# Attention's weighted sum with the values as the stationary operand, and the division by the weights' sums put off until x is loaded

## The chip, the cores and the metric

The kernel runs on one core of a Trainium2 chip. The metric is device time in microseconds of one execution; the kernel before has a median of 813.89 us over three runs (812.94 to 816.54). Engines are TensorE (PE), VectorE (DVE), ScalarE (ACT), GpSimd (POOL) and SyncE (SP), which issues nearly all DMA transfers.

## The reference

Block-sparse attention over 4 batches, 8 heads, 768 positions and 64 values a head, and then a two-layer MLP on the joined heads (3072 tokens, 512 to 2048 to 512). Cut to what matters:

```
scores = scale * q @ k.T                       # scale = 1/8
mask: own block of 32 and its neighbours, first and last block, 3 sampled blocks per query block
      (queries of the first and the last block see every key)
attn = exp(scores - max);  attn = attn / (sum(attn) + 1e-9)
x = (attn @ v), heads side by side             # (3072, 512)
h = x @ w_in;  r = max(h, 0);  g = s * r * r + b;  out = g @ w_out
```

The MLP works on numbers split in a high and a low part, with three products for one.

## The kernel before

**Slots.** The attention runs over 52 slots in the order `T["ORD"]`, two batches (a and b) at a time. An "s" slot is four heads against one tile of 128 queries; its keys are 256 local and global ones (the static part) and, for each block of 32 queries, three sampled blocks (the sampled part). There are 40 of them. A "d" slot (8) does the first and last query block, with all 768 keys, for two pairs of heads; an "h" slot (4) does the half tile that is left at the end of a batch, for all eight heads. A unit is one tile of weights within a slot: four to an "s" or "h" slot, two to a "d" slot.

**Work of a slot.** PE makes scores (L710, L724, sampled L736). DVE adds the mask and takes the maximum (L751), ACT exponentiates and leaves the sum of each row in `dn` (L763). PE transposes the weights (L787), DVE and ACT in turn copy them out of PSUM (L791, L793). PE multiplies with the values: static part L832 ("d" L821, "h" L826), sampled part L846. Here the transposed weights are the stationary operand, 64 queries of them in the static part and 32 in the sampled one, and 64 columns of V move, so that the result has queries on partitions. `x_scale` (L852, DVE) multiplies it by the reciprocals that `recip` (L766) made of the slot's sums; `x_transpose` (L858, PE) turns it, two 128x128 pieces for an "s" or "h" slot and one for a "d" slot; `x_copy` (L863, ACT) takes it out of PSUM, and `spill` (L875) stores it to `xd` in DRAM. The result and its transpose share one PSUM bank, of which there is one for all slots; seven others hold scores and transposed weights.

**The order.** Class `Plan` holds each step of the attention, of the decoding of the weights w_in and w_out (64-bit words, nine steps on DVE and ACT for a block, L75 to L85) and of the first 30 MLP sub-steps as an op with an engine, a cost, a priority and its dependencies. `Plan.order` simulates the engines and writes every engine's instructions in the order that comes out; each engine then runs its own queue in that order. The PE sequence of the attention is fixed by `line`: weights' transposes of slot i, x transposes of slot i-1, scores of slot i+2, products of slot i.

**The MLP.** x is held in eight halves of 384 tokens (`g` from 0 to 7, two to a batch). `xload` (L359) brings two 128-row pieces of a half from `xd`, and `xsplit` makes the high part on ACT (L372) and the low part on DVE (L374). A sub-step `(g, f)` is the first layer for 128 hidden columns (L401 to L403, four triples), the square and split of the hidden values (L406 to L419), and two sub-steps later the second layer (L440 to L442). Halves 0 and 1 run first, 2 and 3 from sub-step 32; the sub-steps from 30 on are written in a plain loop, not planned. Halves 4 to 7 are done at the end with seven products instead of eight (L1193); they read x through `get` (L1152).

## Time and profile before

| what | value |
|---|---|
| median of three runs | 813.89 us (812.94 to 816.54) |
| the profiled execution | 807.04 us, span 805.3 us |
| busy: PE, DVE, ACT, POOL | 785.4, 560.9, 493.8, 214.6 us |
| DMA | 95.61 MB, mean 119 GB/s |
| granted PE clock, mean | 0.996 |

The attention fills the span up to about 276 us, the planned sub-steps of the MLP the part up to about 400, the loop the part up to about 540, and the last four halves the rest. Rows give start, length, engine and line, tiles written and read, the number of instructions in brackets or after an x, and in square brackets the idle time before and what ended it. A PE row counts matmuls, a PEld row the loads of the stationary operand, which overlap them. In groups by line the first number behind the bar is busy time in us, the second the mean length of one in ns.

### The profile page before, as it was taken

What the parts mean: (1) busy time and instruction counts of PE and PEld (TensorE: products, weight loads), DVE (VectorE), ACT (ScalarE), POOL (GpSimd) and SP (SyncE); (2) the same over time, 40 slices, a digit from 0 to 9 for tenths busy, and PEclk for the clock granted to TensorE, in tenths of its full rate; (3) what the DMA queues carried; (4) which work ended last, traced back from release to release, by engine and by line L of the source; (5) the groups of instructions that cost most, each with busy time, mean ns of one, the idle gap of its engine ahead of it and who ended that gap; (6) DMA issues with size and microseconds to landing.
All of it is one profiled execution on the core that took longest, in us unless ns stands there. A gap on an engine that the chain in (4) does not pass through costs nothing.

```text
span 805.3 us, 22018 instructions
## 1 busy us (share of the span) xinstructions
PE 785.4 (98%) x8416; PEld 682.0 (85%) x8416; DVE 560.9 (70%) x1379; ACT 493.8 (61%) x1175; POOL 214.6 (27%) x438
## 2 busy tenths in 40 slices
PE   8988999999999999999999999999999999999997
PEld 6677887888887889999889999998899998999996
DVE  4756778888888899999742222278768869766662
ACT  3656778878788788787563433457355457544542
POOL 1732133222400032322323222223223223322321
PEclk9999999999999999999999999999999999999999
DMA  8988897887777433433221010412200012000002
GB/s 257 279 226 294 229 258 214 251 247 222 210 221 230 142 105 105 132 105 109 81 98 40 30 37 27 158 46 78 86 1 7 0 40 95 6 1 0 1 2 78
DMA packets 86073, 95.61 MB, mean 119 GB/s; under 512 B 11344, under 2 KB 64976, under 8 KB 85968
## 3 DMA queue, kind: packets, MB, share of 16 engines
q1 hardware_dynamic: 85968, 94.21, 38.6%
q8 instruction: 66, 1.08, 0.6%
q14 instruction: 39, 0.32, 0.1%
HBM read 77.41 MB, written 12.58 MB: 112 GB/s over the span
## 4 chain that ended last, share of the span: by engine, by line
PE 85%; ACT 4%; DMA 4%; DVE 3%; issue 3%; SPq 1%; POOL 0%; ACTq 0%; DVEq 0%; POOLq 0%
PE m L1193 13%; PE o L441 10%; PE o L442 10%; PE o L440 10%; PE t L787 9%; PE xs L832 5%; PE s L710 5%; PE h L402 5%; PE h L403 5%; PE h L401 5%; PE xs L846 3%; PE s L736 2%; PE s L724 2%; PE xs L858 1%; PE xs L821 1%
## 5 line engine op out<-in xcount | busy, mean ns | idle before, releaser
L419 POOL TENSOR_TENSOR hid<-hid,hid 128x384 fp32r<-128x384 f32 x128 | 139.3, 1089 | 436.5 <-ACT hid L415 253.2
L763 ACT ACTIVATE ptile<-ptile,nm 128x352 f32<-128x352 f32 (+2 forms) x208 | 120.8, 583 | 30.7 <-DVE nm L751 29.7
L1210 ACT ACTIVATE hid<-hid,sb_b,sb_s 128x384 f32<-128x384 f32 x64 | 45.4, 709 | 112.4 <-DVE hid L1204 112.3
L410 DVE SCALAR_TENSOR_TENSOR hid<-hid,sb_s 128x384 f32<-128x384 f32 x64 | 41.5, 649 | 88.4 <-ACT hid L406 88.3
L670 POOL COPY kg<-kt 128x128 f32 x264 | 63.5, 293 | 124.4 <-PE s L736 119.0
L751 DVE CUSTOM_DVE_ANT_0 ptile<-s,ms 128x352 f32<-128x352 f32 x160 | 74.4, 521 | 25.6 <-PE s L736 25.4
L401 PE MATMUL h<-x,win 128*128 128x384 f32 x256 | 86.5, 338 | 0.6 <-ACT hid L406 0.6
L402 PE MATMUL h<-x,win 128*128 128x384 f32 x256 | 86.1, 336 | 0.2 <-DVE x L374 0.2
L403 PE MATMUL h<-x,win 128*128 128x384 f32 x256 | 86.3, 337 | 0.0
L787 PE MATMUL t<-ident,ptile 128*128 128x128 f32 x608 | 79.4, 280 | 0.7 <-ACT ptile L763 0.7
L442 PE MATMUL o<-woutr,hid 128*128 128x512 f32 x192 | 75.9, 395 | 0.0
L442 PE MATMUL o<-wout,hid 128*128 128x512 f32 x192 | 75.9, 395 | 0.0
L441 PE MATMUL o<-wout,hid 128*128 128x512 f32 x192 | 75.8, 395 | 0.0
L441 PE MATMUL o<-woutr,hid 128*128 128x512 f32 x192 | 75.8, 395 | 0.0
L440 PE MATMUL o<-wout,hid 128*128 128x512 f32 x192 | 74.7, 389 | 0.0
L440 PE MATMUL o<-woutr,hid 128*128 128x512 f32 x192 | 74.6, 389 | 0.0
L787 PEld LDWEIGHTS t<-ident,ptile 128*128 128x128 f32 x608 | 65.9, 141 | 6.9 <-ACT ptile L763 1.9
L406 ACT ACTIVATE hid<-h 128x384 f32<-128x384 f32 x64 | 31.1, 486 | 52.3 <-PE h L403 49.2
L414 ACT ACTIVATE hid<-hid,sb_b 128x384 f32<-128x384 f32 x64 | 39.3, 614 | 37.8 <-DVE hid L410 37.8
L791 DVE COPY pt<-t 128x384 f32<-128x384 f32 (+1 forms) x104 | 56.1, 545 | 8.1 <-PE t L787 5.6
L793 ACT COPY pt<-t 128x384 f32<-128x384 f32 (+1 forms) x104 | 48.8, 472 | 20.9 <-PE t L787 20.3
L1193 PE MATMUL m<-xT,wop 128*128 128x384 f32 x288 | 58.5, 337 | 2.6 <-DVE sum L1286 1.5
(169 smaller groups left out, 1650.8 us busy)
## 6 DMA issues: line engine op xcount, KB each, us to landing
vg<-in_v_dram SPq DMA_DIRECT2D x136, 128.0 KB, 3.7
v<-in_v_sta_dram SPq DMA_DIRECT2D x40, 256.0 KB, 4.7
kt<-in_k_seq_dram SPq DMA_DIRECT2D x16, 544.0 KB, 7.0
raw_i<-in_w_in_dram SPq DMA_DIRECT2D x16, 512.0 KB, 4.9
raw_o<-in_w_out_dram SPq DMA_DIRECT2D x16, 512.0 KB, 3.3
v<-in_v_dram SPq DMA_DIRECT2D x16, 384.0 KB, 5.0
xd<-xst SPq DMA_DIRECT2D x44, 128.0 KB, 4.0
out_dram<-ob SPq DMA_DIRECT2D x20, 256.0 KB, 2.1
```

The source lines that it names most:

```text
L401: nc.tensor.matmul(ph, wh, xh, start=(c == 0), stop=False)
L402: nc.tensor.matmul(ph, wh, xl, start=False, stop=False)
L403: nc.tensor.matmul(ph, wl, xh, start=False, stop=(c == NCC - 1))
L419: nc.gpsimd.tensor_tensor(out=htile(5 + i % 3), in0=t, in1=gh.bitcast(F32), op=ALU.subtract)
L440: nc.tensor.matmul(acc, gh[:, tsl], wout(f, 0), start=first, stop=False)
L441: nc.tensor.matmul(acc, gh[:, tsl], wout(f, 1), start=False, stop=False)
L442: nc.tensor.matmul(acc, gl[:, tsl], wout(f, 0), start=False, stop=last)
L670: nc.gpsimd.tensor_copy(kg[:, m], kts[b][:, :, bass.ds(box["js"][m], BLK)])
L751: nc.vector.tensor_tensor_reduce(out=pt[:, :w], in0=sps.pop((n, g))[:, :w], in1=msk, scale=-scale, scalar=FMAX if g == 0 else nm[:, 0:1], ...
L763: nc.scalar.activation(pt[:, :w], pt[:, :w], AF.Exp, bias=nms[n][:, last:last + 1], scale=-1.0, accum_out=dns[i][:, g, j:j + 1])
L787: nc.tensor.transpose(tp[:, c, :], src[:, c * P:(c + 1) * P], ident)
L1193: nc.tensor.matmul(to, w_, x_, start=(c == 0 and k == 0), stop=(c == 1 and k == 2))
```

## The change

In the product with the values the operands change places. V is stationary (64 columns of one head) and the transposed weights move: 128 queries at a time in the static part, 32 in the sampled part, two heads of a pair on the two halves of the output partitions. The result then has the head's values on partitions and queries along the free dimension, as x is stored, and `x_transpose` goes; `x_copy` moves it from PSUM on DVE. A slot's result is not divided. The sums of a batch are gathered in one tile of 52 columns (`sums`); when its last slot has its exponentials, `recip` makes reciprocals of them, PE transposes them, and 48 rows of 128 are stored to `rd` in DRAM. Whoever loads a piece of x also loads the matching factors, repeated over 64 partitions (`rload`: two transfers for an even half, six for an odd one), and `xscale` multiplies in place, 128x768 on DVE. Halves 4 to 7 are loaded, multiplied and stored back to `xd` in sub-steps 34 to 49 (`xback`). The factors for halves 0 and 1, and the raw x of half 1, lie in a tile of their own (`xr`), which takes a turn in the two buffers of the sampled values. The planner's costs are set anew.

```diff
+    def rload(g, c2, t):
+        b, hf = divmod(g, 2)
+        t3 = t.rearrange("p (t c n) -> p t c n", c=2, n=P)
+        nt = HALF // P - hf
+        for par in range(2):
+            to = t3[par * D:(par + 1) * D]
+            o = (24 + par * 8 if hf else par * 12)
+            src = rd[b, o:o + 4 * nt].rearrange("(t x) n -> t x n", x=4)[:, 2 * c2:2 * c2 + 2, :].rearrange("t x n -> t (x n)")
+            nc.sync.dma_start(out=to[:, :nt].rearrange("p t c n -> p t (c n)"), in_=src.unsqueeze(0).broadcast_to([D, nt, 2 * P]))
+            if hf:
+                src = rd[b, 40:48].rearrange("(h r k) (a n) -> r k a h n", r=2, k=2, a=2)[par, c2]
+                for a in range(2):
+                    nc.sync.dma_start(out=to[:, nt, a].rearrange("p (h n) -> p h n", h=2), in_=src[a].unsqueeze(0).broadcast_to([D, 2, D]))
+        rfac[(g, c2)] = t
+    def xscale(g, c2, dst=None):
+        t = xraw[(g, c2)] if dst is None else dst
+        nc.vector.tensor_tensor(out=t, in0=xraw[(g, c2)], in1=rfac[(g, c2)], op=ALU.mult)
+        xraw[(g, c2)] = t
+    def xback(g, c2):
+        nc.sync.dma_start(out=xd[g // 2, g % 2, :, :, 2 * c2:2 * c2 + 2, :], in_=tcn(xraw[(g, c2)]))
...
-                                 accum_out=dns[i][:, g, j:j + 1])
-        def recip(i):
...
+                                 accum_out=sums[slots[i][1]][:, sum_column(n, g):sum_column(n, g) + 1])
+        def recip(b):
+            t = sums[b]
+            nc.vector.tensor_scalar(out=t[:, :NROW], in0=t[:, :NROW], scalar1=1e-9, scalar2=None, op0=ALU.add)
+            nc.vector.tensor_tensor(out=t[:, NROW - 4:NROW], in0=t[:, NROW - 4:NROW], in1=t[:, NROW:], op=ALU.add)
+            nc.vector.reciprocal(t[:, :NROW], t[:, :NROW])
+        def recip_transpose(b):
+            tps[("r", b)] = next_bank(f"r{b}")[:NROW, :P]
+            nc.tensor.transpose(tps[("r", b)], sums[b][:, :NROW], ident)
...
-            hp = 2 * (j % 2) + j // 2
-            for c in range(2):
-                for rows in halves:
-                    nc.tensor.matmul(xs[rows], pt[:, c, rows], vt[:, c, hp * D:(hp + 1) * D], start=(j == 0 and c == 0),
-                                     stop=False, skip_group_check=True)
+            for c in range(2):
                 for par in range(2):
+                    j = 2 * k + par
+                    pt = pts_of[n + j][0]
...
+                        hp = 2 * par + k
+                        to, w, p = xs[halves[par], k], vt[:, c, hp * D:(hp + 1) * D], pt[:, c, :]
+                    nc.tensor.matmul(to, w, p, start=(k == 0 and c == 0), stop=False, skip_group_check=True)
...
-                    nc.tensor.matmul(xs[rows], w, vg[:w.shape[0], m, h * D:(h + 1) * D], start=False, stop=(j == 3),
-                                     tile_position=(0, r * BLK), skip_group_check=True)
+            for k in range(2):
                 for r in range(4):
+                    for par in range(2):
...
+                        nc.tensor.matmul(to, vg[:p.shape[0], m, h * D:(h + 1) * D], p, start=False, stop=(k == 1 and r == 3),
+                                         tile_position=(0, par * D), skip_group_check=True)
-        def x_scale(i):
...
-        def x_transpose(i):
...
-            nc.scalar.copy(xst_of[i], tr)
+            nc.vector.tensor_copy(xst_of[i], xs)
...
-        costs = {"s": (485, 535, 350, 260, 685), "d": (810, 0, 350, 780, 0), "h": (380, 535, 240, 160, 685)}
+        costs = {"s": (485, 535, 350, 470, 640), "d": (810, 0, 350, 1420, 0), "h": (380, 535, 240, 240, 640)}
...
             for c2 in range(2):
                 xload(2, c2)
+                rload(2, c2, scratch("klp", HX, f"r2_{c2}").bitcast(F32))
         mlp1(i)
         if i in (31, 32):
+            for c2 in range(2):
+                xscale(i - 29, c2)
             for c in range(NCC):
                 xsplit(i - 29, c)
         if i == 31:
             for c2 in range(2):
                 xload(3, c2)
+                rload(3, c2, scratch("khp", HX, f"r3_{c2}").bitcast(F32))
...
+        if 34 <= i < 50:
+            m, k = divmod(i - 34, 2)
+            gc = 4 + m // 2, m % 2
+            if k == 0:
+                xload(*gc)
+                rload(*gc, scratch("klp", HX, f"r{gc}").bitcast(F32))
+            else:
+                xscale(*gc)
+                xback(*gc)
```

**PE, the products of one "s" slot.** Before (`v` and `vg` are the static and the sampled values, `pt` the transposed weights, `xs` the result):

```order
L832 MATMUL xs_2434<-v_0_2075,pt_0_2391 64x64 x4
L832 MATMUL xs_2434<-v_0_2075,pt_0_2397 64x64 x4
...
L846 MATMUL xs_2434<-vg_2_1469,pt_0_2391 32x64 x4
L846 MATMUL xs_2434<-vg_2_1469,pt_0_2397 32x64 x4
...
L787 MATMUL t_0_2547<-ident,ptile_81 128x128 x3
L858 MATMUL xs_2434<-ident,xss_2544 128x128 x2
```

Now, with the two heads in turn (8 rows of the first kind, 16 of the second):

```order
L878 MATMUL xs_2009<-pt_0_1973,v_0_1791 64x128
L878 MATMUL xs_2009<-pt_0_1979,v_0_1791 64x128
...
L893 MATMUL xs_2009<-pt_0_1973,vg_2_1366 64x32
L893 MATMUL xs_2009<-pt_0_1979,vg_2_1366 64x32
...
L833 MATMUL t_0_2079<-ident,ptile_81 128x128 x3
```

The sizes are the output's partitions and columns. 16 static products of 64 moving columns have become 8 of 128, 16 sampled ones of 64 columns on 32 partitions have become 16 of 32 columns on 64, and the two transposes behind the next slot's are gone.

**DVE, from the last copies of transposed weights to the first MLP sub-steps.** Before (`win` and `wout` are decoded blocks, `wkhp`, `wklp` and `raw` their steps, `hid` the hidden values):

```order
L791 COPY pt_0_6987<-t_0_6973 128x384
L85 SCALAR_TENSOR_TENSOR win_5488<-wklp_2714,wkhp_2704 128x512
L78 SCALAR_TENSOR_TENSOR wklp_2715<-wklp_2715,raw_i_6167 128x512
L83 TENSOR_TENSOR win_5488<-wkhp_2705,raw_i_6167 128x512
L84 TENSOR_SCALAR wkhp_2705<-win_5488 128x512
L852 TENSOR_TENSOR xss_7033<-xs_7000,rc_6983 128x128
L85 SCALAR_TENSOR_TENSOR win_5488<-wklp_2715,wkhp_2705 128x512
```

Now:

```order
L837 COPY pt_0_6293<-t_0_6280 128x384
L401 TENSOR_TENSOR x_1_6001<-xraw_1_4465,x_0_5857 128x384 x2
L83 TENSOR_TENSOR win_5116<-wkhp_2726,raw_i_5517 128x512
L383 TENSOR_TENSOR xr<-xr 128x768
L901 COPY xst_6339<-xs_6298 128x128
L819 COPY rt_6346<-r_6327 48x128
L383 TENSOR_TENSOR xr<-xr 128x768
L401 TENSOR_TENSOR x_1_6361<-xr,x_0_6341 128x384
L437 SCALAR_TENSOR_TENSOR hid_6359<-hid_6359,sb_s 128x384
L401 TENSOR_TENSOR x_1_6361<-xr,x_0_6341 128x384 x3
```

Two low parts of half 0 and all four of half 1 (L401, before L374), and both multiplies of half 1 (L383), now stand behind the last copy; before, the six low parts stood ahead of it. Up to the first block of `wout` there are five squares in both orders.

**SP, the loads for halves 2 and 3.** Before:

```order
L359 DMA xraw_0_8138<-xd 128x3x256
L359 DMA xraw_1_8140<-xd 128x3x256
L359 DMA xraw_0_8183<-xd 128x3x256
L359 DMA xraw_1_8185<-xd 128x3x256
L451 DMA out_dram<-ob_0_8228 128x512
```

Now, from the last of these loads on:

```order
L362 DMA xraw_1_7530<-xd 128x3x256
L374 DMA r_1_7532<-rd 64x2x256
L378 DMA r_1_7532<-rd 64x2x64 x2
L374 DMA r_1_7532<-rd 64x2x256
L378 DMA r_1_7532<-rd 64x2x64 x2
L478 DMA out_dram<-ob_0_7582 128x512
```

Six transfers of factors have come between the last load of x and the first store of output; the other three loads have two, two and six behind them.

More of the change, by code (lines that the diff above doesn't have):

```diff
@@ L818, in av_static @@
                 for c in range(NCH):
-                    for par in range(2):
-                        rows = halves[par]
-                        nc.tensor.matmul(xs[rows], pt[c // 3][:, c % 3, rows], vt[:, c, rows], start=(c == 0), stop=(c == NCH - 1))
+                    for a in range(2):
+                        for j in range(2):
+                            nc.tensor.matmul(xs[halves[j], a], vst[(i, j)][:, c, halves[a]], pts[j][c // 3][:, c % 3, halves[a]],
+                                             start=(c == 0 and a == 0), stop=(c == NCH - 1 and a == 1), skip_group_check=True)
@@ L849, in x_scale @@
-        def x_scale(i):
-            xs = xs_of.pop(i)
-            xss = xss_of[i] = xp.tile([P, 4, D], F32, tag="xss", name=f"xss{i}")[:, :xs.shape[1], :]
-            nc.vector.tensor_tensor(out=xss, in0=xs, in1=rcs.pop(i).unsqueeze(2).broadcast_to(list(xs.shape)), op=ALU.mult)
-        def x_transpose(i):
-            tr = tr_of[i]
-            xv = xss_of.pop(i).rearrange("p h d -> p (h d)")
-            for pr in range(tr.shape[1]):
-                nc.tensor.transpose(tr[:, pr, :], xv[:, pr * P:(pr + 1) * P], ident)
@@ L1036 @@
         o_t, o_av, ends = last[1][-1], last[2][-1], [y for x in evs.values() for y in x]
-        every = [ac, o_av, *ends]
+        every = [ac, o_av, *ends, rt[len(slots) - 1]]
         op("s", 450, 30, lambda: nc.sync.dma_start(out=sb_s, in_=s_in.rearrange("(a o) -> a o", o=1).broadcast_to([P, 1])))
```

174 lines of the change are left out of this document (95 added, 79 removed).

## The prediction

> **What bounds the kernel now.** I read the page first (busy shares, then the 40 slices), then the chain of waits between 78 and 274 us, then busy time by stage, and last the two places where one stage hands over to the next.
>
> ```profile
> PE 785.4 (98%) x8416; PEld 682.0 (85%) x8416; DVE 560.9 (70%) x1379; ACT 493.8 (61%) x1175; POOL 214.6 (27%) x438
> PE   8988999999999999999999999999999999999997
> DVE  4756778888888899999742222278768869766662
> ```
>
> TensorE (PE) is full from the fourth slice on. VectorE (DVE) is full beside it in slices 15 to 20, about 280 to 400 us. The chain says what PE's time consists of. This is one "s" slot (four heads against 128 queries) of the attention:
>
> ```profile
> 84.43 0.49 PE s L736 x32
> 84.93 1.08 PE xs L832 x32
> 86.01 0.58 PE xs L846 x32
> 86.59 1.46 PE t L787 x12
> 88.05 0.22 PE xs L858 x2
> 88.27 1.06 PE s L710 x8
> ```
>
> Six groups, 4.9 us, no gap: in this stage the other engines' savings are worth nothing, and only PE's own steps count. Before about 78 us it is different; the chain there has pieces like these, in which PE waits for loads:
>
> ```profile
> 34.44 7.30 DMA v<-in_v_dram
> 44.35 4.57 DMA vg<-in_v_dram
> ```
>
> Only 6 of the 40 "s" slots lie there (192 of 1280 records, 32 to a slot):
>
> ```profile
> L832 PE MATMUL xs<-v,pt 128*64 128x64 f32 x192 | 7.2, 226 | 1.0 <-issue 1.0
> ```
>
> In the MLP, PE is busy all 20 us of each stretch, and DVE has 0.6 to 1.9 us left in it (columns: PE, PEld, DVE, ACT, POOL busy):
>
> ```profile
> 300.00:320.00 20.00, 20.00 (x103) 18.21 (x102) 18.11 (x31) 15.51 (x28) 5.57 (x5) 1.00 0.27 82
> 340.00:360.00 20.00, 20.00 (x101) 18.04 (x101) 19.38 (x32) 15.19 (x27) 5.46 (x5) 1.00 0.39 124
> ```
>
> **The step price on PE.** The program has 16 static products to a slot and the trace 32 matmuls with 32 weight loads, so each product is two of each. The old static products alternate between two halves of the array, so 32 are 16 steps. Two groups of the same shape but different count separate the step from what a change of shape costs, and the weight loads show how long one takes:
>
> ```profile
> 263.50 1.55 PE xs L821 x48
> 128.87 0.62 PE xs L826 x16
> 130.07 1.02 PE t L787 x8
> L710 PEld LDWEIGHTS s<-kt,qr_4s 64*128 64x128 f32 x64 | 5.5, 186 | 1.7 <-issue 1.3
> L832 PEld LDWEIGHTS xs<-v,pt 128*64 128x64 f32 x1280 | 40.7, 138 | 7.8 <-issue 1.1 <-ACT ptile L763 0.6 <-ACT pt L793 0.6
> L846 PEld LDWEIGHTS xs<-vg,pt 96*32 96x32 f32 x1280 | 20.2, 109 | 6.0 <-issue 3.3
> ```
>
> 24 steps take 1.55 and 8 take 0.62, so a step is (1.55 - 0.62) / 16 = 0.058 us and a group's fixed part 0.62 - 8 x 0.058 = 0.16. Twelve transposes take 1.46 and eight 1.02, so 128 moving columns cost 0.11, and 64 some 0.055. A load grows from 109 ns at 32 stationary columns to 186 at 128: 0.8 ns a column, so 64 columns occupy about 51 ns. In the old static step load (51) and stream (55) overlap.
>
> **Part 1: the new products.** Static: 8 products with 128 moving columns are 8 steps of 0.11 plus 0.16, 1.04 us instead of 1.08. Sampled: the stationary side is now 64 columns of V and the moving side 32 queries, on two halves instead of four quarters, so 16 steps instead of 8. Each streams 0.11 / 4 = 0.0275 us but loads 64 columns. Bounds: 0.0275 if the loads hide, 0.051 + 0.0275 = 0.079 if nothing overlaps. I take 0.058, the step of the rows that load 64 columns every time: the stream is shorter there, the load is not. That is 16 x 0.058 = 0.93 us, and no fixed part, since static and sampled now have one shape, against 0.58. The two L858 transposes (0.22) go. A slot: 1.08 + 0.58 + 0.22 = 1.88 becomes 1.04 + 0.93 = 1.97, +0.09; 34 slots make +3.1. An "h" slot: 0.62 + 0.58 + 0.22 becomes 0.62 + 0.93, +0.13, four make +0.5. A "d" slot has 24 steps of the same load before and after and loses one transpose: -0.11, and the four late ones make -0.4. Four transposes of the sums: +0.4; the one of the third batch stands right behind the slot whose sums it needs and waits for three small DVE operations, about 0.2 each: +0.6. Sum for PE: **+4.2 us**.
>
> A rule speaks against the sampled half as well: the Trainium skill, TensorEngine Tiling, "Instruction Overhead", says that a matmul with one moving column takes as long as one with 60. By it a step would be 60 / 128 x 0.11 = 0.052 and the sampled group 0.83 us, an estimate, 0.1 below mine; no row here has 32 moving columns.
>
> **Part 2: what leaves DVE and ACT.**
>
> ```profile
> L852 DVE TENSOR_TENSOR xss<-xs,rc 128x256 f32<-128x256 f32 x44 | 18.6, 423 | 7.0 <-PE xs L846 6.9
> L863 ACT COPY xst<-xs 128x256 f32<-128x256 f32 x44 | 16.4, 372 | 17.5 <-PE xs L858 16.0 <-DMA vg<-in_v_dram 0.7 <-DMA v<-in_v_sta_dram 0.3
> L775 DVE RECIPROCAL rc<-rc 128x4 f32<-128x4 f32 x44 | 7.8, 178 | 1.5
> L774 DVE TENSOR_SCALAR rc<-dn 128x4 f32<-128x4 f32 x44 | 7.4, 168 | 0.0
> ```
>
> The multiply of 0.42 becomes a copy of the same shape; ACT's copies and the small reciprocals go, some 16 and 15 us of busy time. All of it lies beside the full PE: worth 0. The copy sits under the next slot's transposes and scores, 1.46 + 1.06 us; without that cover it would cost 0.42 a slot.
>
> **Part 3: the handover to the MLP.** The division comes back as xscale, a 128x768 multiply on DVE, ahead of every split of x. For the second half of batch 0 it comes after the last attention copy, so that six splits and two multiplies stand between it and the first decoded block of w_out, which the first second-layer product needs:
>
> ```profile
> L1166 DVE TENSOR_TENSOR sum<-sum,sum 128x768 f32<-128x768 f32 x6 | 5.7, 950 | 0.0
> 271.60 1.01 DVE L374 TENSOR_TENSOR x<-wout,x 128x384 fp32r<-128x384 f32 x2
> 274.42 0.54 DVE L791 COPY pt<-t 128x384 f32<-128x384 f32 x1
> 290.49 0.69 DVE L85 SCALAR_TENSOR_TENSOR wout<-wklp,wkhp 128x512 fp32r<-128x512 f32 x1
> L83 DVE TENSOR_TENSOR win<-wkhp,raw_i 128x512 fp32r<-128x512 f32 x16 | 12.1, 759 | 1.3 <-ACT wkhp L82 0.7 <-issue 0.4 <-ACT raw_i L79 0.2
> 275.36 1.62 PE L821 MATMUL xs<-v,pt 128*64 128x64 f32 x48
> 287.80 0.44 PE L401 MATMUL h<-x,win 128*128 128x384 f32 x1 [0.60 <-ACT hid L406]
> 291.04 0.40 PE L440 MATMUL o<-wout,hid 128*128 128x512 f32 x1
> ```
>
> Before, DVE needs 291.2 - 275.0 = 16.2 us from the last copy to that block. In the same stretch of the changed order stand six splits more (0.5 each, from the pair that takes 1.01: 3.0), two multiplies (0.95 each: 1.9), and a net half microsecond of decode steps (one L83 more, one L78 for one L84) and of copies: +5.5, so 21.7. PE's cover is the last slot's product (1.55) and first-layer products: before, 26 triples in 291.04 - 276.91, less 0.6 of wait and 0.1 of transpose, so 0.515 each; in the changed order 28 stand ahead. PE is out of work 1.55 + 0.1 + 14.4 = 16.1 us after that product starts, the block is ready 21.7 - 0.4 = 21.3 after: a stall of 5.2 where there were 0.6, **+4.6**. PE cannot make it up, being full afterwards. Bounds: 0 if DVE closes the gaps of its 16.2 us, 7 if the added operations run with the contention that made some there twice as long.
>
> **Part 4: the third and fourth x at sub-steps 31 and 32.** Here the split was just in time:
>
> ```profile
> 407.54 0.52 SPq L359 DMA_DIRECT2D xraw<-xd  x1
> 411.80 0.45 PE L402 MATMUL h<-x,win 128*128 128x384 f32 x1 [0.23 <-DVE x L374]
> win<-xrest SPq DMA_DIRECT2D x30, 128.0 KB, 2.0
> xd<-xst SPq DMA_DIRECT2D x44, 128.0 KB, 4.0
> ```
>
> The load at 407.54 waits for a buffer of the x before. Behind it SP now issues six more transfers for the factors, 0.5 each: the last at 411.4, landed at 413.4 (2.0, as transfers of this quiet stretch) to 415.4 (4.0). On DVE both multiplies stand ahead of all four splits, so the first split ends 0.95 + 0.55 later, at 414.9 to 416.9, and PE waits for it instead of until 411.80; behind it wait the square of that sub-step and, on SP, the output stores, both with microseconds to spare. +3.1 to +5.1, and I take **+3.6**, near the row of the quiet stretch. The eight scalings with write-back from sub-step 34 on fall into slices where DVE is at 2 to 4 tenths, and cost nothing; were DVE full there, they would cost 8 x 0.95.
>
> **Sum.** 4.2 + 4.6 + 3.6 = 12.4 us. The profiled execution took 807.0 us (span 805.3), so 819.4 in its terms. The three timed runs have a median of 813.9, 0.85% above it; taken to the median, 826.
>
> **Rivals.**
> Loads hide (faster): if a load runs ahead under other matmuls, the sampled step is 0.0275, its group 0.44, and a slot loses 0.40: 34 x 0.40 + 4 x 0.36 + 0.4 - 1.0 = 14.4 less on PE, and with parts 3 and 4 a net -6: 808. It decides below a step of about 0.042. For it: load and stream overlap in L832 today. Against it: they overlap one deep, the step there is 0.058 with a load of 0.051, and in the new step nothing is left to overlap with. The Trainium skill, TensorE: Matmul & The Clock Gate, "The mechanism", speaks for this rival: the queue pulls a load ahead of running matmuls where it goes to another part of the array or to the background buffer.
> Only PE's part shows (no change): DVE catches up before the first w_out block, and the factors land in time; +4.2, 818.
> The queue hurts more (slower still): the new order puts one k block and two tiny loads ahead of the v load of the third slot, in the stage where the chain runs through DMA; 3 us there, with the upper bounds 7 and 5.1: +19, 833.
> That the change does not do what it says is excluded by the order of PE's rows: the transposes are gone and the shapes are as described.
>
> **Chances.** Forecast 0.55, loads hide 0.12, only PE's part 0.17, worse 0.16. Faster or slower means by over 0.5%, about 4 us, what a measurement of this kernel can tell: below 809.8 is the first rival alone, 0.12; the second lies at the edge of 818 and counts as no change with a little of the others, 0.18; slower 0.70. Range 808 to 834; the forecast's own is 820 to 831.
>
> **What would show it.** Right: in the chain, the new sampled group at about 0.93 us with 32 records and the static one at 1.04; a period of about 5.0 us; a PE wait of some 5 us for the first w_out block and one of 3 to 5 us at the second x of sub-step 33, named DVE. Wrong: a sampled group of 0.5 us, a DVE that finishes the block within 17 us, or an x split on time. The forecast falls if the sampled step is below 0.042.

## The result

The changed kernel takes 827.13 us (median of 4 runs, 825.7 to 828.67), the kernel before 815.21 (812.94 to 817.32). The ratio is 1.0153 with a 95% interval of 1.011 to 1.0197: slower by about 12 us. The forecast was 826.

The profiled execution of the changed kernel has a span of 824.1 us, 18.8 more than the first profile of before (805.3). A second profile of before, taken later, has 811.9, much nearer to its median. So every place is compared with both. The stretches between fixed points on PE (slots counted from 0 to 51, MLP sub-steps from 0 to 63; the start of the first matmul of each) are, in us:

| stretch | before | before, second profile | changed |
|---|---|---|---|
| start to the scores of slot 7 | 51.3 | 54.9 | 53.3 |
| to the scores of slot 48 | 201.1 | 202.6 | 199.7 |
| to the first layer of sub-step 8 (the handover) | 52.2 | 52.2 | 61.0 |
| to sub-step 32 | 102.45 | 102.45 | 102.45 |
| to sub-step 38 (the joins of the third and fourth x) | 25.6 | 25.6 | 31.95 |
| to sub-step 62 (multiplies with write-back) | 100.5 | 100.5 | 103.45 |
| to the end | 272.1 | 273.7 | 272.2 |

Three stretches are longer, by 8.8, 6.3 and 3.0 us, together 18.1; the attention up to slot 48 is not longer at all in this execution (in others with the same product it is, see experiment 3). The page of the changed kernel shows the first two of them as notches in PE's slices, the 14th with the 15th and the 21st, where before had nines:

```profile
PE 793.1 (96%) x7684; PEld 693.1 (84%) x7684; DVE 568.6 (69%) x1307; ACT 479.9 (58%) x1123; POOL 215.7 (26%) x438
PE   8799999999999879999979999999999999999997
```

**The slot.** The chain of waits of the changed kernel (start, length, group) shows five groups, 4.95 us from the scores of one slot to those of the next (a period below) where before had six groups and 4.90:

```profile
58.33 1.06 PE s L737 x8
59.40 0.49 PE s L763 x32
59.89 1.02 PE xs L878 x16
60.91 0.91 PE xs L893 x32
61.82 1.46 PE t L833 x12
```

**The handover.** PE's timeline (in brackets the idle time ahead and what ended it):

```profile
272.91 0.27 PE L815 MATMUL r<-ident,sums 128*48 128x128 f32 x1 [1.19 <-DVE sums L811]
279.31 0.44 PE L428 MATMUL h<-x,win 128*128 128x384 f32 x1 [0.69 <-DVE rt L819]
293.42 0.45 PE L428 MATMUL h<-x,win 128*128 128x384 f32 x1 [1.35 <-ACT hid L433]
298.48 0.49 PE L467 MATMUL o<-wout,hid 128*128 128x512 f32 x1 [2.71 <-DVE wout L83]
299.67 0.77 PE L468 MATMUL o<-wout,hid 128*128 128x512 f32 x1 [0.69 <-DVE wout L85]
300.24 0.63 PE L469 MATMUL o<-wout,hid 128*128 128x512 f32 x1
300.67 0.63 PE L467 MATMUL o<-wout,hid 128*128 128x512 f32 x1
```

Two of the waits are the sums (their inversion on DVE, and the copy of their transpose, whose bank the first MLP product wants), two are the first block of w_out, and the one of 1.35 us is for a hidden value on ACT. The products behind them start 0.43 us apart instead of 0.23: PE's clock is lower there, 0.61 in the first of the stretches that follow.

**The joins.** In busy time by stretch (PE, PEld, DVE, ACT, POOL, then the granted clock, DMA share, GB/s) both notches end in a piece with a clock of 0.6, with 10 and 13 matmuls where the next piece of the same length has 18 and 22:

```profile
300.00:304.00 4.00, 3.74 (x10) 2.60 (x10) 3.33 (x7) 3.94 (x7) 0.00 (x0) 0.61 0.39 124
304.00:308.00 4.00, 4.00 (x18) 3.31 (x19) 3.93 (x7) 3.08 (x7) 1.30 (x1) 1.00 0.45 132
426.00:430.00 4.00, 3.88 (x13) 3.84 (x14) 2.00 (x5) 3.52 (x9) 0.42 (x1) 0.57 0.43 167
430.00:434.00 4.00, 4.00 (x22) 3.65 (x21) 0.62 (x1) 3.19 (x6) 0.90 (x2) 1.00 0.57 204
```

The second notch is the fourth x, in the timelines of PE, DVE and SP's queue:

```profile
426.12 0.69 PE L429 MATMUL h<-x,win 128*128 128x384 f32 x1 [4.85 <-DVE x L401]
426.92 0.52 PE L428 MATMUL h<-x,win 128*128 128x384 f32 x1
427.24 0.52 PE L429 MATMUL h<-x,win 128*128 128x384 f32 x1
```
```profile
418.65 0.94 DVE L383 TENSOR_TENSOR xraw<-xraw,r 128x768 f32<-128x768 f32 x1
424.63 0.96 DVE L383 TENSOR_TENSOR xraw<-xraw,r 128x768 f32<-128x768 f32 x1 [5.04 <-DMA r<-rd]
425.51 1.96 DVE L401 TENSOR_TENSOR x<-xraw,x 128x384 fp32r<-128x384 f32 x4
```
```profile
417.29 0.54 SPq L362 DMA_DIRECT2D xraw<-xd  x1
420.78 1.81 SPq L378 DMA_DIRECT2D r<-rd  x2
```

SP's load of the second piece waits for a buffer until 417.29; the six transfers of its factors stand behind it, the last landed at 424.63, and all four splits, those of the first piece too, wait on DVE behind the second multiply.

**The multiplies with write-back.** At sub-steps 47 and 49 DVE waits for the factors in the same way and holds up the square that is next in its queue (509.53 in the second case), and PE waits four times, for 0.21 and 0.41 us near 502 and for 0.89 and 0.40 near 512. By the starts of the matmuls around them, which lie 1.2 and 1.8 us further apart than elsewhere, these waits are the whole 3.0 us. The longest is shown last:

```profile
498.45 0.96 DVE L383 TENSOR_TENSOR xraw<-xraw,r(7, 0)_8072 128x768 f32<-128x768 f32 x1 [5.48 <-DMA r(7, 0)_8072<-rd]
508.65 0.96 DVE L383 TENSOR_TENSOR xraw<-xraw,r(7, 1)_8141 128x768 f32<-128x768 f32 x1 [5.97 <-DMA r(7, 1)_8141<-rd]
509.53 0.61 DVE L437 SCALAR_TENSOR_TENSOR hid<-hid,sb_s 128x384 f32<-128x384 f32 x1
```
```profile
511.39 0.50 PE L467 MATMUL o<-woutr,hid 128*128 128x512 f32 x1 [0.89 <-ACT hid L442]
```

### The profile page after: what moved, and what is told of

Same layout as the page of the kernel before. It is cut to its first block, busy times and chain, and to the rows that moved or that the text cites. A ratio compares the mean times of both kernels' runs of the same rounds, so it can differ in the third digit from the quotient of the medians.

```text
span 824.1 us, 20594 instructions
## 1 busy us (share of the span) xinstructions
PE 793.1 (96%) x7684; PEld 693.1 (84%) x7684; DVE 568.6 (69%) x1307; ACT 479.9 (58%) x1123; POOL 215.7 (26%) x438
## 4 chain that ended last, share of the span: by engine, by line
PE 69%; DVE 16%; ACT 5%; DMA 5%; SPq 3%; issue 2%; POOL 0%; DVEq 0%; ACTq 0%
PE m L1246 13%; PE t L833 8%; PE o L469 7%; PE o L468 7%; PE o L467 7%; PE xs L878 5%; PE s L737 5%; PE xs L893 5%; PE s L763 3%; DVE hid L437 2%; PE h L429 2%; PE h L430 2%; PE h L428 2%; DMA kt<-in_k_seq_dram 2%; DVE wkhp L84 2%
## 5 line engine op out<-in xcount | busy, mean ns | idle before, releaser
L441 ACT ACTIVATE hid<-hid,sb_b 128x384 f32<-128x384 f32 x64 | 39.3, 614 | 65.5 <-DVE hid L437 65.5
L437 DVE SCALAR_TENSOR_TENSOR hid<-hid,sb_s 128x384 f32<-128x384 f32 x64 | 44.1, 689 | 47.6 <-ACT hid L433 47.6
L839 ACT COPY pt<-t 128x384 f32<-128x384 f32 (+1 forms) x104 | 48.6, 469 | 39.3 <-PE t L833 38.9
L1246 PE MATMUL m<-win 128*128 128x384 f32 x288 | 55.9, 338 | 0.0
```

The lines of the kernel that those rows point to most:

```text
L1246: nc.tensor.matmul(to, w_, x_, start=(c == 0 and k == 0), stop=(c == 1 and k == 2))
```

## The experiments

The theory after the result: the product costs almost nothing, and the division put off costs nearly all. The rivals: the product or its layout costs; the multiplies' own time costs; the loads cost; the order that the planner wrote costs.

**1. The kernel before once more.** No edit.

> The kernel before, unchanged, profiled a second time. The profiled execution of before took 807.0 us while its timed runs had a median of 815.2; the changed kernel's profiled execution took 825.9 and its median was 827.1. So the profiles differ by 18.8 us and the medians by 11.9. If the first profile of before was a lucky execution, this one has a span near 812 to 815 and shows by name a stretch that is some 8 us longer than in the first (I expect it where the kernel is just in time: the split of x before 411.8 us, where PE waited 0.23 us, and the loads before 78 us). If executions with a profile are simply shorter for this kernel, the span is 804 to 807 again and nothing moves.

Span 811.9, 813.67 us by the clock. The 6.6 us more lie in the loads before slot 7 (3.6), in waits between slots 7 and 48 (1.5 more than in the first profile) and, at the end, in the clock: the same PE wait of 1.5 us near 555 us is followed by a full clock in the first profile of before and by 3.4 us of slow clock in the second (10 matmuls against 17):

```profile
554.00:557.40 3.40, 3.40 (x17) 3.01 (x18) 2.41 (x5) 2.45 (x6) 2.02 (x2) 1.00 0.00 0
```
```profile
559.00:562.40 3.40, 3.35 (x10) 3.06 (x11) 2.43 (x5) 2.56 (x6) 1.89 (x2) 0.57 0.00 0
```

So the first profile of before was a lucky one, and not at the split before 411.8 us, where I had looked for it: that stretch is the same to 0.03 us. The stretches marked 52.2, 102.45, 25.6 and 100.5 repeat so well that they are used below.

**2. Without the division, order kept.**

```diff
     def rload(g, c2, t):
+        return
...
-        nc.vector.tensor_tensor(out=t, in0=xraw[(g, c2)], in1=rfac[(g, c2)], op=ALU.mult)
-        xraw[(g, c2)] = t
+        return
...
-        if 34 <= i < 50:
+        if False:
```

> The changed kernel without the put-off division: no loads of the factors, no multiply of x, no write-back of the scaled x; x stays undivided (so the result leaves the division out). The transposed products stay, and so does the order of everything else. Theory (the put-off division costs 17.4 of the 18.8 us between the two profiles, the transposed product 1.4): first second-layer product at 291 to 293 us instead of 298.5, no PE wait of more than 0.5 us between 415 and 430 and none between 500 and 515, span 806 to 809, and timed 0.98 to 1.00 of before. Rival (the transposed product, its layout in memory or the new order of the loads is what costs): the span stays above 818 and the waits of the changed kernel stay.

Ratio 1.0037 (1.0005 to 1.0069), span 814.6, both above the theory's. The joins are whole again (25.6 and 100.5), as the theory had it. The handover is not: 61.6 us, and the first second-layer product at 296.2. My account of the handover (VectorE has 1.9 us of multiplies and 3.0 of splits more to do) falls as far as the multiplies go. They are gone, and PE waits the same; DVE, in order, now stands waiting for the first square (the first three rows give what PE waited for: us in total, times, longest):

```profile
PE o L467 <- DVE wout L83: 2.7, 1, 2.7
PE h L428 <- ACT hid L433: 1.4, 1, 1.4
PE r L815 <- DVE sums L811: 1.2, 1, 1.2
```
```profile
279.95 0.62 DVE L437 SCALAR_TENSOR_TENSOR hid<-hid,sb_s 128x384 f32<-128x384 f32 x1 [2.50 <-ACT hid L433]
```

**3. Multiplies, but no loads of factors.** In each multiply the second operand is x itself (the result is x squared); `rload` returns at once.

```diff
-        nc.vector.tensor_tensor(out=t, in0=xraw[(g, c2)], in1=rfac[(g, c2)], op=ALU.mult)
+        nc.vector.tensor_tensor(out=t, in0=xraw[(g, c2)], in1=xraw[(g, c2)], op=ALU.mult)
```

> The changed kernel with the multiplies of x and the write-back, but without the loads of the factors: each multiply takes x itself as its second operand (the result is x squared instead of x divided). It parts the DVE work of the put-off division from the loads that it waits for. Theory: the handover (8.1 us in the profile) is DVE work and stays, first second-layer product at 297 to 299 us; the PE wait of 4.85 us at 421 and the waits of 1.7 us at 501 to 512 are loads of the factors, and go: span 813 to 816. Rival (the multiplies themselves, ahead of the splits and of the squares, make all three): the wait at 421 stays above 3 us, those at 501 to 512 stay, span 821 to 824.

Ratio 1.0077 (1.0046 to 1.0108), span 820.8. Handover 61.0, as expected; the joins 26.75, a wait of 1.12 us left of 4.85; sub-steps 38 to 62 back at 100.5. So of the 6.3 us at the fourth x the multiplies make 1.1 and the loads 5.2, and the 3.0 behind are loads alone. The span is 5 us above what I gave, nearly all of it before slot 48: the two periods from the scores of slot 24 to those of slot 26 are together 5.9 us too long. PE waits there for the sampled values:

```profile
141.21 1.28 PE L893 MATMUL xs<-pt,vg 96*64 96x32 f32 x20 [2.44 <-DMA vg<-in_v_dram]
```

The last two loads of these values (issued at 137.3 and 137.9 us) stand behind a store of x in SP's queue; in before they stand ahead of it. And this is not one execution's accident. Over the twelve profiles with the transposed product, these two periods are 2.6 to 6.1 us too long in six, 1.2 to 1.4 in two, and at most 0.7 in four, the changed kernel's own among them; in the two profiles of before it is at most 0.5. So the change has a cost here that comes and goes and that the table above does not show. What decides whether it comes stays open.

**4. Half the stationary columns in the sampled product.**

```diff
-                        nc.tensor.matmul(to, vg[:p.shape[0], m, h * D:(h + 1) * D], p, start=False, ...
+                        nc.tensor.matmul(to[:D // 2], vg[:p.shape[0], m, h * D:h * D + D // 2], p, start=False, ...
```

> The changed kernel with 32 instead of 64 stationary columns of V in each sampled product (the second half of each head's dimensions is left out of the sampled part); count, moving columns and everything else are as in the changed kernel. Theory (a step of the sampled group is as long as its weight load, 0.057 us for 64 columns): with 32 columns the load is some 0.026 us, the stream of 32 moving columns 0.0275, a step 0.028 to 0.035, the sampled group 0.45 to 0.56 us instead of 0.91, the slot 4.5 to 4.6 us instead of 4.95, and the attention ends 13 to 17 us earlier. Rival (a matmul with few moving columns has a floor, as the Trainium skill, TensorEngine Tiling, 'Instruction Overhead', states; the floor would be 0.052 us by 60 columns): the group stays at 0.83 to 0.91 and the slot above 4.85.

PE's timeline in the changed kernel (first two rows) and here:

```profile
59.82 1.09 PE L878 MATMUL xs<-pt,v 128*64 128x128 f32 x16
60.74 1.08 PE L893 MATMUL xs<-pt,vg 96*64 96x32 f32 x32
```
```profile
161.16 1.53 PE L833 MATMUL t<-ident,ptile 128*128 128x128 f32 x12
164.17 1.09 PE L878 MATMUL xs<-pt,v 128*64 128x128 f32 x16
165.20 0.70 PE L893 MATMUL xs<-pt,vg 96*32 96x32 f32 x32
165.83 1.53 PE L833 MATMUL t<-ident,ptile 128*128 128x128 f32 x12
```

The slot is 4.67 us instead of 4.95. The 32 sampled matmuls are 16 steps of two side by side. From their first start to their last end they take 0.70 us instead of 1.08; less the last one's own length (0.20 and 0.22), that is 0.033 a step instead of 0.057. The moving columns are the same 32, so the stationary columns set the step. 24 ns less for 32 columns less is close to the 0.8 ns a column of the prediction, and the loads themselves take 112 ns instead of 138, 0.8 a column too. The step is what the theory gave (0.028 to 0.035); the slot is not (4.5 to 4.6), because the sampled group now starts 1.03 us after the static one instead of 0.92. These two groups no longer have one shape here; whether that is the reason is not shown. The Trainium skill, TensorEngine Tiling, "Instruction Overhead", has one moving column take as long as 60; read as a floor of the step, an estimated 0.052 us, it does not show, since the step is 0.033. The attention won less than expected (slot 7 to slot 48: 198.9 us against 199.7), because three of the periods between slots 21 and 25 are 2.6 to 4.0 us too long. Timed, nothing is seen (1.0126, 1.0056 to 1.0197).

**5. The multiplies and splits of batch 0's second half early.** One due time, on the multiply and on both split parts:

```diff
-                xm[(g, c2)] = op("v", 950, N + T["XP"] + g * 16, ...
+                xm[(g, c2)] = op("v", 950, N + T["XP"] - g * 112, ...
```

> The changed kernel with one thing moved: the planner's due times of the multiplies and splits of batch 0's second half lie before the end of the attention instead of after it. From the last attention copy to the first decoded block of w_out, VectorE then has 25 instructions in its order (no split, no multiply) instead of 37 (six splits, two multiplies); the kernel before has 26. Measure: from the start of the last attention slot to the first-layer product of sub-step 8, 38.0 us in before, 46.9 in the changed kernel, 47.5 without any multiply (order unchanged), 46.9 without loads. Theory (the place of the splits in VectorE's order makes the handover, not the multiplies' time): 38 to 40 us, slots of the attention stay at 4.95, the two late waits (6.3 and 3.0 us) stay, span 814 to 818 in an execution like the changed kernel's. Rival (VectorE's work is only moved; in the attention it delays the maxima and so PE): the slots from 220 us on lengthen by 4 us or more in sum and the span stays above 820.

Slower: 1.0194 (1.0155 to 1.0233), span 831.4. The rival is right. The handover, measured from the last slot, is 39.3 us as the theory said, but the last three periods between scores take 12.3, 7.0 and 7.0 us instead of 4.8, 4.8 and 4.5. DVE stands 3.4 us on the factors ahead of the maxima, PE waits 3.0, and the clock is halved for some ten microseconds:

```profile
257.38 0.96 DVE L383 TENSOR_TENSOR xr<-xr 128x768 f32<-128x768 f32 x1 [3.40 <-DMA xr<-rd]
```
```profile
259.43 1.55 PE L751 MATMUL s<-kt,qr_5d 64*64 64x384 f32 x4 [3.03 <-DVE pt L837]
```
```profile
255.00:260.00 5.00, 1.97 (x14) 0.70 (x16) 2.62 (x6) 2.12 (x5) 0.00 (x0) 0.93 0.59 169
260.00:265.00 5.00, 5.00 (x55) 4.03 (x52) 2.74 (x10) 2.55 (x8) 0.00 (x0) 0.50 0.96 303
265.00:270.00 5.00, 4.86 (x24) 2.70 (x22) 3.00 (x8) 1.68 (x4) 0.00 (x0) 0.55 0.29 89
```

**6. The factors' loads ahead of time.**

```diff
-            for c2 in range(2):
-                xscale(i - 29, c2)
             for c in range(NCC):
+                if c % 2 == 0:
+                    xscale(i - 29, c // 2)
                 xsplit(i - 29, c)
...
-            for c2 in range(2):
-                xload(3, c2)
-                rload(3, c2, ...)
+            xload(3, 0)
+            for c2 in range(2): rload(3, c2, ...)
+            xload(3, 1)
...
-        if 34 <= i < 50:
+        if 34 <= i < 52:
...
-            else:
-                xscale(*gc)
-                xback(*gc)
+            elif m:
+                xscale(4 + (m - 1) // 2, (m - 1) % 2)
+                xback(4 + (m - 1) // 2, (m - 1) % 2)
```

> The changed kernel with the loads of the factors no longer just in time in the MLP: (1) the factors of the fourth x are loaded ahead of its second load, which waits for a buffer, and each half of x is multiplied right before its own two splits; (2) the eight later multiplies with write-back come two sub-steps later than now, three after their loads. Theory (VectorE, in order, waits for a load and holds up the split and the squares behind it): the PE wait of 4.85 us at 421 falls to 1.5 or less with no slow clock behind it (6.3 falls to 2 or less), the 3.0 us at 501 to 512 go, the handover of 46.9 us stays; span 815 to 818. Rival (the transfers themselves are too slow there, or SP's queue is what is late): the wait at 421 stays above 3 us, the later ones move on by two sub-steps.

Ratio 1.0062 (1.0033 to 1.0091), span 821.9. (The last multiply is made twice here and in the next run.) The span misses the theory. The 3.0 us are gone. The wait of 4.85 became three of 0.73, 0.36 and 0.73, but the stretch to sub-step 38 is 30.1, not the 27.6 or less of the theory: short as the waits are, the clock dropped behind them too (0.57), and 3.6 us brought 10 matmuls instead of 19:

```profile
427.80:431.40 3.60, 3.55 (x10) 3.08 (x11) 1.46 (x3) 3.55 (x8) 0.75 (x1) 0.57 0.56 218
431.40:435.00 3.60, 3.60 (x19) 3.35 (x18) 0.68 (x1) 2.39 (x5) 0.81 (x2) 0.96 0.60 212
```

**7. Both together.**

> The two edits of the runs beside this one together: the splits of batch 0's second half early, and the factors' loads ahead of time. Theory: what is left of the change is the product, 0.05 us a slot, and the transposes of the sums: 2 to 3 us; span 806 to 812, timed 0.995 to 1.005 of before. Rival (the two are not independent: what is won at the handover is lost at the next place that is just in time): span above 815, timed above 1.008.

1.0117 (1.0077 to 1.0157), span 822.6: the rival. The handover from slot 48 is 66.8, worse than 61.0; what the loop won, the early splits lost.

**8. The order without the division.** As experiment 2, and the planner's costs of the loads and multiplies set to 1 ns.

> As the run without the division (no factor loads, no multiplies, no write-back), but the planner too is told that they cost nothing, so that it makes its order without them: 19 instructions on VectorE from the last copy to the first block of w_out, and 48 first-layer matmuls ahead of the first second-layer product instead of 84. Theory (the handover's 8.9 us are made by the order that the planner wrote for the costs it was given; taking the work away and leaving the order gained nothing, 47.5 us): 38 us or less from the start of the last slot to the product of sub-step 8; span 804 to 808 in an execution like the one without the division, timed 0.99 to 1.00 of before. Rival (the transposed layout or the late sums make the handover): stays above 44 us.

0.9962 (0.9938 to 0.9986), span 810.0. From slot 48 the handover is 57.5 us: with the same work left out, the order alone is worth 4.1 (61.6 before). That is less than the theory, which wanted all of the 8.8 (38 us or less from the last slot; it took 43.3). In what is left, PE waits 2.2 us for a copy behind the sums' three operations on DVE, and the first MLP product 0.7 for the sums' copy:

```profile
269.93 2.24 PE L865 MATMUL xs<-pt,v 128*64 128x64 f32 x46 [2.24 <-DVE pt L837]
281.43 0.45 PE L428 MATMUL h<-x,win 128*128 128x384 f32 x1 [0.71 <-DVE rt L819]
```

**9. All work kept, four joins moved.** Experiment 6, with these:

```diff
-                xm[(g, c2)] = op("v", 950, N + T["XP"] + g * 16, ...
+                xm[(g, c2)] = op("v", 950, N + T["XP"] + g * -40, ...
-                        ... order=ox, nbytes=393e3, **(use or {"use": [xkey]}))
+                        ... order=ox, nbytes=393e3, late=4000.0, **(use or {"use": [xkey]}))
-                o = op("v", 500, u + nu + T["RP"], lambda b=b: recip(b), [o_e])
+                o = op("v", 500, u + nu + T["RP"], lambda b=b: recip(b), [o_e], order=[o_ev])
-            if i - 1 in rt:
-                line.append(rt[i - 1])
...
             line += tensor[i][2]
+            if i - 1 in rt: line.append(rt[i - 1])
...
+        relu(i)
-        if i in (31, 32):
+        if i in (30, 32):
...
-            elif m:
+            elif k and m:
```

The due time is changed for the multiplies alone; the splits keep theirs.

> The changed kernel, all its work kept and every result divided, with its four joins moved: (1) the multiplies and splits of batch 0's second half have a due time before the end of the attention, and the planner is told that the factors land 4 us later than its model says (in the run with early multiplies VectorE stood 3.4 us on that load and held up the maxima); (2) the sums of a batch are inverted after the last copies of their slot, and their transpose on PE stands one slot later; (3) the third x is multiplied and split before the square of sub-step 30 instead of after it, each half of an x right before its two splits, and the fourth x's factors are loaded ahead of its second load; (4) the later multiplies come three sub-steps after their loads. In the run beside this one's forerunner the last multiply was made twice; here once. Theory (the product costs 0.05 us a slot, all else is waits at these places): from the start of the last slot to the first second-layer product 24 to 26 us (31.3 in the changed kernel, 24.5 in before, 24.1 with the planner told of no division), no PE wait above 0.5 us between 410 and 430 or between 500 and 515, span 806 to 811, timed 0.994 to 1.003 of before. Rival (each removed wait is replaced by one at the next just-in-time place, as with the early multiplies): span above 815, timed above 1.008.

1.0105 (1.0072 to 1.0138), span 824.2: the rival again. The joins take 28.9 and the stretch behind them 100.5, but the moved multiplies and splits crowd DVE in the last slots, and PE waits there instead (2.1 us at 266, 3.1 at 282); the handover is 63.0.

```profile
266.27 0.66 PE L878 MATMUL xs<-pt,v 128*64 128x128 f32 x8 [2.08 <-DVE pt L837]
282.39 0.30 PE L865 MATMUL xs<-pt,v 128*64 128x64 f32 x2 [3.12 <-DVE x L401]
```

**10. The wait filled with matmuls.**

```diff
-        ph = hid[i]
+        ph = hid[i]; i == 33 and [nc.tensor.matmul(ph, win(0, 0)[:, :P], xsp[(2, 0)][:, 0, :], start=True, stop=True) for _ in range(24)]
```

> The changed kernel with 24 more matmuls on PE (128x384, into the bank that the next product overwrites) ahead of the first-layer product of sub-step 33, where PE waits 4.6 to 4.9 us for the second x's split; they use operands that are there. Behind that wait the trace shows eleven matmuls at 0.32 us instead of 0.174. Theory (the slow clock comes from PE's idle time, so the wait costs more than its length): the added matmuls take 24 x 0.174 = 4.2 us inside the wait, the split comes when it came, and the products behind it run at 0.174 at once: from the first-layer product of sub-step 32 to that of sub-step 34 15.2 us less 1.3 to 1.6; the span falls by 1.3 to 1.6 from what it would be, too little for the timed runs. Rival (the slow clock there has another cause, or more matmuls only delay): the matmuls behind the wait stay at 0.32, and the stretch is as long or longer.

The added matmuls take 4.35 us, a wait of 0.55 is left of 4.85, and the products behind run at full clock. From the first layer of sub-step 32 to that of sub-step 34 it took 15.20 us in the changed kernel and 13.63 here, 24 matmuls more in less time by 1.57: without the idle time the slow clock does not come.

```profile
424.23 4.35 PE L424 MATMUL h<-x,win 128*128 128x384 f32 x24
429.30 0.45 PE L429 MATMUL h<-x,win 128*128 128x384 f32 x1 [0.55 <-DVE x L401]
```
```profile
428.00:432.00 4.00, 3.45 (x19) 3.05 (x18) 3.17 (x6) 3.20 (x7) 0.00 (x0) 1.00 0.12 47
```

Timed (1.0132, 1.0084 to 1.0181) it is not told from the changed kernel, as expected.

**11. The product alone.** Experiment 8 without the inversion, transpose and store of the sums.

```diff
-            if all(sl[1] != b for sl in slots[i + 1:]):
+            if False:
```

> The transposed product alone: no factor loads, no multiplies, no write-back, and now also no inversion, transpose and store of the sums, with the planner told of none of them (the division is left out). One stretch is the same in every execution of a kernel: from the scores of the fourth slot before the end of the attention to the first-layer product of sub-step 8 it took 52.2 us in both profiles of before, 61.0 to 61.7 in four profiles with the changed kernel's order there, 61.6 without the multiplies' work, 57.5 with an order made without the division but with the sums. Theory (what is left of the 57.5 is the sums: three small VectorE operations ahead of the copies, two transposes, and a first-layer product that waits for the bank of the second one): 52 to 54 us, timed 0.990 to 0.997 of before. Rival (it is the new product or its order: the nine first-layer matmuls that before had ahead of its last product are behind it in this order too): 56 to 58 us, timed 0.995 to 1.000.

0.9918 (0.9892 to 0.9945), 809.41 us, span 804.6: faster than before by 0.8%. The handover is 51.3 us, below the 52.2 of before and below my 52 to 54. The last product ends and the MLP begins without a pause, in the chain:

```profile
275.04 1.61 PE xs L865 x46
276.65 0.37 PE h L428
```

**12. The changed kernel with the loads mended.** Experiment 6 with the third x before the square of sub-step 30, the activation (`relu`) ahead of these splits, the fourth x loaded one sub-step earlier and every multiply made once.

```diff
+        relu(i)
-        if i in (31, 32):
+        if i in (30, 32):
...
-            elif m:
+            elif k and m:
```

> The changed kernel with every result divided, and only the factors' loads in the MLP ahead of time: the third x multiplied and split before the square of sub-step 30, the fourth x's factors loaded ahead of its second load, the later multiplies three sub-steps after their loads. Order and work up to sub-step 29 are the changed kernel's. Theory: the stretch at the handover stays at 61 us, the 6.3 us at the second x of sub-step 33 fall to 3 or 4 (3.3 in the run with all joins moved), the 3.0 at 501 to 512 go: 5 to 6 us less than the changed kernel, timed 1.005 to 1.010 of before. Rival (the loads are late in profiled executions alone): timed above 1.012.

1.0068 (1.0036 to 1.0101), 821.41 us, span 821.3: half of the loss is back, and this is the best version found that divides every result. It does not beat the kernel before. At the joins 30.4 us are left, 4.8 too many instead of the 3 or 4 expected: the splits wait for ACT's high parts, which stand behind an activation in ACT's queue. The handover takes 62.7 us here, though the order up to it is the changed kernel's; over the executions with that order it is 61.0 to 62.7.

**The ladder.** Each row adds one thing to the row above:

| kernel | time by the kernel before | handover | to sub-step 38 | to 62 |
|---|---|---|---|---|
| product alone (11) | 0.9918 (0.9892 to 0.9945) | 51.3 | 25.6 | 100.5 |
| and the sums inverted and stored (8) | 0.9962 (0.9938 to 0.9986) | 57.5 | 25.6 | 100.5 |
| and the order that the whole change gives (2) | 1.0037 (1.0005 to 1.0069) | 61.6 | 25.6 | 100.5 |
| and the multiplies (3) | 1.0077 (1.0046 to 1.0108) | 61.0 | 26.75 | 100.5 |
| and the factors' loads: the change | 1.0153 (1.011 to 1.0197) | 61.0 | 31.95 | 103.45 |

The second row holds the sums' work and the order that it brings along; these were not parted. The multiplies' step lies within the intervals, and the first two rows touch. The rows come from several sets of runs, beside which the kernel before had medians of 814.1 to 818.1 us, and each carries the waits of experiment 3; so steps of less than some 4 us are told by the stretches and not by the times.

## Why the prediction was right, and where it was not

The time (826 for 827.1), the sign and the range held. The sum behind it held only in part: one term too high and three too low. That 826 came out so near is partly luck. The three places cost 18.1 us where the sum had 4.6, 3.6 and nothing, and the product, counted with the sums at +4.2, alone makes the kernel some 6 us faster; the errors cancel.

- **The step price: right.** Sampled group 0.91 for 0.93, static 1.02 for 1.04, slot 4.95 for 4.99. That the stationary and not the moving columns set the step is shown by experiment 4, and the 0.8 ns a column holds there; the first rival (loads hide, step 0.0275) is out.
- **Part 1 as a sum, +4.2: wrong.** Product alone, the kernel is faster than before, 0.7 us in the profile and 0.8% by time. The step that failed is "all of it lies beside the full PE: worth 0" (part 2): the slot's own groups cost 0.05 more (0.09 in the sum), yet the 41 slots to slot 48 are not longer (201.0 us for the product alone, 201.1 and 202.6 before). PE's idle time among them is 3.0 and 4.3 us in before, 2.6 with the product alone and 1.0 in the changed kernel, so waits have gone; whether through less work on DVE and ACT or through the new order was not parted. Where all of the timed gain of some 6 us comes from stays open; the profiles, 804.6 against 805.3 and 811.9, show no single place.
- **The sums, 0.4 + 0.6: mis-sized.** I counted four transposes and one wait. With the order that they bring, they cost 6.2 us at the handover (51.3 to 57.5).
- **Part 3, the handover, +4.6: right place, wrong cause, too small.** It is 8.8. The wait for the first block of w_out, priced at some 5, is 2.7 and 0.7. By the ladder the sums (the 6.2 above, not to be added again) and the rest of the order (4.1) make the stretch longer. The multiplies' 1.9 us, counted as DVE work, are worth nothing (experiment 2). The step that failed is the sum of DVE's work between two points: DVE's queue waits within it for squares, so what counts is the order. It was also taken for granted that a stall costs its length; the slow clock behind it adds to it.
- **Part 4, the joins, +3.6: right mechanism, mis-sized.** 6.3, of which loads 5.2 and multiplies 1.1. Sub-step 32 starts 9.5 us later than in before (416.5 for 407.0), and with that taken off nearly all came as forecast: the load that waits for a buffer at 407.8 (407.5), the last factor at 415.1 (413.4 to 415.4), PE's product at 416.6 (414.9 to 416.9). The size was taken near the lower bounds. SP needed 4.7 us for the six transfers, not 3.3, so that PE waits 4.6 us more than before. The term that is missing is the slow clock behind the wait, 1.6 (experiment 10).
- **"The eight scalings cost nothing": wrong.** 3.0 us. I looked at DVE's share of busy time, 2 to 4 tenths, and not at what stands behind a multiply that waits for its load: the square, on the same queue.
- **The third rival's early loads:** slot 7 starts at 51.3 and 54.9 us in before and at 53.3 in the changed kernel: nothing to be seen. What a load's place in SP's queue does cost shows later, at slot 24, in some executions (experiment 3); the prediction has no term for that place.

## What to carry to other kernels

Before work is put off, look at the queue in which it will wait: here 0.95 us of multiply cost little, and the loads that it waits for, on an engine that runs in order, cost PE about 8 us at places where that engine has little else to do. A stall costs more than its length where PE's clock falls behind it. Where a planner writes the order, taking work out of the kernel does not show what the work costs; take it out of the plan as well.

## What the runs showed of the hardware

- After a wait PE's clock may fall, to nearly half, for about 3.4 us: eleven products 0.32 us apart instead of 0.17 between 426.1 and 429.5 behind a wait of 4.85, gone when the wait is filled (experiment 10). The Trainium skill, TensorE: Matmul & The Clock Gate, "What's actually happening", says that the array runs at half clock after an idle window of about 3.4 us and until a busy one has passed, and that the windows run freely. The length agrees. But waits much shorter than a window did it too: 1.5 us in one profile of before and not in the other, and 0.73, 0.36 and 0.73 within some 7 us (experiment 6).
- An fp32 product with 32 moving columns has a step of 0.057 us with 64 stationary columns and 0.033 with 32, two such products running side by side (experiment 4).
